# A range flag gathered by a DMA transfer, a fallback program that leaves two engines out, and a last store on another queue

## The chip, the cores and the metric

The kernel runs on one core of a Trainium2 chip, launched as one program. A core has five instruction streams that run on their own and meet through semaphores: TensorE (PE in the profile, with its weight loads as PEld), VectorE (DVE), ScalarE (ACT), GpSimd (POOL) and SyncE (SP), which only issues transfers. The metric is the device time of one execution in microseconds (us); the figure compared is the median of several runs.

## The reference

Two layers follow one another. Inputs are float32: `q`, `k`, `v` of 8 batches x 8 heads x 576 tokens x 64, and the weights of a mixing MLP.

```python
k_p = k.reshape(B, H, 72, 8, D).mean(axis=3)          # pooled keys, 72 of them
v_p = v.reshape(B, H, 72, 8, D).mean(axis=3)
scores = scale * np.matmul(q, k_p.transpose(0, 1, 3, 2))
attn = np.exp(scores - np.max(scores, axis=-1, keepdims=True))
attn = attn / (np.sum(attn, axis=-1, keepdims=True) + 1e-09)
x = np.matmul(attn, v_p)                              # then (B, S, 512)
a1 = alpha1 * x + beta1
u = x + lam * np.einsum('ts,bsd->btd', w_tok, a1)     # mixes the tokens
a2 = alpha2 * u + beta2
out = u + lam * (np.maximum(a2 @ w_ch1, 0.0) @ w_ch2) # 512 -> 2048 -> 512
```

## The kernel before

There are two programs in the kernel. `direct` (line 181) is the fast one. It takes the exponentials without subtracting the maximum, so it is exact enough only while the sums of exponentials stay in a certain range. `general` (line 24) subtracts the maximum, in plain float32, and is there for inputs that leave this range. `tile_pooling_attn__then__resmlp_affine_kernel` (line 1207) runs `direct`, reads a count that `direct` leaves in SBUF into a register of each engine (`values_load`, line 1215), and runs `general` under `tc.If(good < P)` (line 1216). With the inputs measured here the count is 128 and `general` is jumped over: its instructions lie in the instruction streams of the engines, between the last instruction of `direct` and the end of the program, and every engine that takes part in the `If` reads the count, compares and branches past them.

`direct` splits the 8 x 576 tokens into 36 chunks of 128 (the ninth chunk of two batches holds the two remainders of 64 tokens) and the chunks into 9 blocks of four, n = 0 to 8. A block goes through the MLP: `mlp_A` (line 832) makes the hidden layer `H` by 64 products of 128x512 a block, each relu'd by ScalarE (line 850); for blocks from `FIRST` on the second layer is a Winograd-like scheme of seven half-size products instead of eight, with sums of `H` by VectorE (`hidden_sum`, line 925), the products on TensorE (`product`, line 939, line 966) and the sums into the result tile `u_sb` by VectorE (`gather`, lines 981 and 984). While block n is in the MLP, the attention of batch n + 1 runs between its products. The order is written out by hand: each block makes a list `todo` of (due time, step), sorts it and emits the steps in that order (line 1202); inside `direct` the engines keep that order.

The last block, n = 8, has no attention beside it. What matters in its list:

- At 1.5 `all_in_range` (line 227): four VectorE instructions test the reciprocals of all sums (`recs`, 128 x 320) and reduce them to `each`, 128 x 1, one flag in each partition.
- At 7.2 `count_in_range` (line 238): a TensorE product of `each` with a column of ones (`ones_fp`) in a PSUM tile of the pool `gp` gives the number of good partitions, and VectorE converts it to the int32 `count`.
- From 16 on the products, in the order 1, 2, 6, 5, 7, 4, 3, each of the two row pairs `pp` by itself.
- The stores of the result by `store` (line 874), which writes one chunk by one transfer (line 879) or, for the chunk of remainders (m = 3), two transfers of 64 rows (line 883). At 19.1 the left halves of the chunks m = 0 and 1, at 25.2 the right halves of m = 2 and 3, at 27.2 the left halves of m = 2 and 3 (line 1171, one of the 64-row transfers from ScalarE), and at 29.2 the right halves of m = 0 and 1 (line 1173):

```python
todo.append((29.2, lambda m=m: store(
    n, m, HALF, DM, ((nc.sync, nc.scalar)[m],) * 2)))
```

So m = 0 is stored by SyncE's queue and m = 1, the very last piece of the result, by ScalarE's.

Behind the `If` stands the end of the program (all of it recorded under line 1243): SyncE waits for the semaphores of all queues and engines one after another, and the five engines meet twice before the program ends. On the way past the body of the `If` each engine also brings the semaphores that the body would have raised to the value that they would have had (instructions EVENT_SEMAPHORE recorded under line 1216): SyncE those of its eight transfer queues, the others their own.

Of the kernel before, what the change touches and what calls it, by code (L numbers as in the profile page):

```python
# [23 lines left out]
def general(  # L24
# [27 lines left out]
    ident = sb.tile([P, P], FP, tag="ident", name="g_ident")  # L52
    nc.vector.memset(ident, 0.0)
    nc.gpsimd.affine_select(out=ident, in_=ident, compare_op=ALU.not_equal, fill=1.0, base=0,
                            pattern=[[-1, P]], channel_multiplier=1)
    pool = sb.tile([P, 16], FP, tag="pool", name="g_pool")
    nc.vector.memset(pool, 0.125)
    nc.gpsimd.affine_select(out=pool, in_=pool, compare_op=ALU.is_ge, fill=0.0, base=0,
# [3 lines left out]
    pools = sb.tile([P, 5, SPG], FP, tag="pools", name="g_pools")  # L62
    nc.vector.memset(pools, 0.0)
    for c in range(5):
        n = 16 if c < 4 else 8
        nc.vector.tensor_copy(out=pools[:, c, 16 * c:16 * c + n], in_=pool[:, 0:n])

    vec = {}
    for name, src in (("a1", alpha1), ("b1", beta1), ("a2", alpha2), ("b2", beta2), ("lam", lam)):
        vec[name] = sb.tile([P, DM], FP, tag=f"vec_{name}", name=f"g_{name}")  # L70
        nc.sync.dma_start(out=vec[name], in_=src.unsqueeze(0).to_broadcast((P, DM)))
    w1 = sb.tile([P, 4, DFF], FP, tag="w1", name="g_w1")
    nc.sync.dma_start(out=w1, in_=w_ch1.rearrange("(c p) j -> p c j", p=P))
    w2 = sb.tile([P, NJ, DM], FP, tag="w2", name="g_w2")
    nc.sync.dma_start(out=w2, in_=w_ch2.rearrange("(j p) d -> p j d", p=P))

# [6 lines left out]
    for c in range(5):  # L83
        n, rows = tok(c)
        w = sb.tile([P, S], FP, tag="w_tok", name="g_w")
        nc.sync.dma_start(out=w[0:n], in_=w_tok[rows])
        for i in range(5):
            m, cols = tok(i)
            nc.scalar.copy(out=wT[0:m, i, rows], in_=transposed(w[0:n, cols], n, m))

    for b in range(B):
        raw = []
        for src in (q, k, v):
            t = sb.tile([P, 5, H, D], FP, tag=f"raw{len(raw)}", name="g_raw")
            for c in range(5):
                n, rows = tok(c)
                nc.sync.dma_start(out=t[0:n, c], in_=src[b, :, rows].rearrange("h p d -> p h d"))
            raw.append(t)
        means = []
        for t in raw[1:]:  # L100
            ps = ps_l.tile([P, DM], FP, tag="l", name="g_pl")
            for c in range(5):
                n, _ = tok(c)
                nc.tensor.matmul(out=ps[0:SPG], lhsT=pools[0:n, c],
                                 rhs=t[0:n, c].rearrange("p h d -> p (h d)"),
                                 start=(c == 0), stop=(c == 4))
            m = sb.tile([SPG, DM], FP, tag=f"mean{len(means)}", name="g_mean")
            nc.vector.tensor_copy(out=m, in_=ps[0:SPG])
            means.append(m)
        kp, vp = means  # L110
        x = sb.tile([P, 5, DM], FP, tag="x", name="g_x")
        for h in range(H):
            cols = slice(D * h, D * h + D)
            kT = tmp.tile([D, SPG], FP, tag="kT", name="g_kT")
            nc.scalar.copy(out=kT, in_=transposed(kp[:, cols], SPG, D))
            for c in range(5):
                n, _ = tok(c)
                qT = tmp.tile([D, P], FP, tag="qT", name="g_qT")
                nc.scalar.copy(out=qT[:, 0:n], in_=transposed(raw[0][0:n, c, h], n, D))
                sc = ps_s.tile([P, P], FP, tag="s", name="g_sc")[0:n, 0:SPG]  # L120
                nc.tensor.matmul(out=sc, lhsT=qT[:, 0:n], rhs=kT)
                col = tmp.tile([P, 4], FP, tag="col", name="g_col")
                nc.vector.tensor_reduce(out=col[0:n, 0:1], in_=sc, op=ALU.max, axis=AX.X)
                E = tmp.tile([P, SPG], FP, tag="E", name="g_E")
                nc.vector.tensor_scalar(out=E[0:n], in0=sc, scalar1=col[0:n, 0:1], scalar2=None,
                                        op0=ALU.subtract)
                nc.scalar.activation(out=E[0:n], in_=E[0:n], func=AF.Exp, bias=0.0, scale=0.125)
                nc.vector.tensor_reduce(out=col[0:n, 1:2], in_=E[0:n], op=ALU.add, axis=AX.X)
                nc.vector.tensor_scalar(out=col[0:n, 2:3], in0=col[0:n, 1:2], scalar1=1e-9,
                                        scalar2=None, op0=ALU.add)  # L130
                nc.vector.reciprocal(out=col[0:n, 3:4], in_=col[0:n, 2:3])
                ET = tmp.tile([SPG, P], FP, tag="ET", name="g_ET")
                nc.scalar.copy(out=ET[:, 0:n], in_=transposed(E[0:n], n, SPG))
                av = ps_s.tile([P, P], FP, tag="s", name="g_av")[0:n, 0:D]
                nc.tensor.matmul(out=av, lhsT=ET[:, 0:n], rhs=vp[:, cols])
                nc.vector.tensor_scalar(out=x[0:n, c, cols], in0=av, scalar1=col[0:n, 3:4],
                                        scalar2=None, op0=ALU.mult)
        a = sb.tile([P, 5, DM], FP, tag="a", name="g_a")
        for c in range(5):
            n, _ = tok(c)  # L140
            nc.vector.tensor_tensor(out=a[0:n, c], in0=x[0:n, c], in1=vec["a1"][0:n], op=ALU.mult)
            nc.vector.tensor_tensor(out=a[0:n, c], in0=a[0:n, c], in1=vec["b1"][0:n], op=ALU.add)
        aT = sb.tile([P, 4, S], FP, tag="aT", name="g_aT")
        for c in range(5):
            n, rows = tok(c)
            ps = ps_l.tile([P, DM], FP, tag="l", name="g_pl")
            for i in range(5):
                m, _ = tok(i)
                nc.tensor.matmul(out=ps[0:n], lhsT=wT[0:m, i, rows], rhs=a[0:m, i],
                                 start=(i == 0), stop=(i == 4))  # L150
            y = tmp.tile([P, DM], FP, tag="y", name="g_y")
            nc.vector.tensor_tensor(out=y[0:n], in0=vec["lam"][0:n], in1=ps[0:n], op=ALU.mult)
            nc.vector.tensor_tensor(out=x[0:n, c], in0=x[0:n, c], in1=y[0:n], op=ALU.add)
            nc.vector.tensor_tensor(out=y[0:n], in0=x[0:n, c], in1=vec["a2"][0:n], op=ALU.mult)
            nc.vector.tensor_tensor(out=y[0:n], in0=y[0:n], in1=vec["b2"][0:n], op=ALU.add)
            for cc in range(4):
                nc.scalar.copy(out=aT[:, cc, rows],
                               in_=transposed(y[0:n, P * cc:P * cc + P], n, P))
# [9 lines left out]
        for c in range(5):  # L168
            n, rows = tok(c)
            ps = ps_l.tile([P, DM], FP, tag="l", name="g_pl")  # L170
            for j in range(NJ):
                nc.tensor.matmul(out=ps[0:n], lhsT=hid[:, j, rows], rhs=w2[:, j],
                                 start=(j == 0), stop=(j == NJ - 1))
            y = tmp.tile([P, DM], FP, tag="y", name="g_y")
            nc.vector.tensor_tensor(out=y[0:n], in0=vec["lam"][0:n], in1=ps[0:n], op=ALU.mult)
            nc.vector.tensor_tensor(out=x[0:n, c], in0=x[0:n, c], in1=y[0:n], op=ALU.add)
            nc.sync.dma_start(out=out[b, rows], in_=x[0:n, c])


@with_exitstack  # L180
def direct(
# [13 lines left out]
    out: bass.AP,  # L195
    count: bass.AP,
):
# [26 lines left out]

    each = const.tile([P, 1], FP, tag="each", name="each")

    def all_in_range():
# [7 lines left out]
        nc.vector.tensor_tensor(out=ok, in0=ok, in1=flat, op=ALU.mult)  # L235
        nc.vector.tensor_reduce(out=each, in_=ok, op=ALU.min, axis=AX.X)

    def count_in_range():

        ps = gp("ps_ok")  # L240
        nc.tensor.matmul(out=ps[0:1, 0:1], lhsT=each, rhs=ones_fp)
        nc.vector.tensor_copy(out=count, in_=ps[0:1, 0:1])

# [142 lines left out]
    nc.vector.memset(ones_row, 1.0)  # L386
    ones_fp = const.tile([P, 1], FP, tag="ones_fp", name="ones_fp")
    nc.vector.memset(ones_fp, 1.0)

# [734 lines left out]
    for n in range(NBLK):  # L1124
# [27 lines left out]
        if n >= FIRST:  # L1152
# [14 lines left out]
            if last:  # L1167
                for m in range(2):
# [4 lines left out]
                    todo.append((29.2, lambda m=m: store(  # L1173
                        n, m, HALF, DM, ((nc.sync, nc.scalar)[m],) * 2)))
            else:
# [31 lines left out]
def kernel(ctx: ExitStack, tc: tile.TileContext, *args):  # L1207
# [4 lines left out]
    held = ctx.enter_context(tc.tile_pool(name="held", bufs=1))  # L1212
    count = held.tile([1, 1], mybir.dt.int32, tag="count", name="count")
    direct(tc, *args, count)
    good = nc.values_load(count[0:1, 0:1], min_val=0, max_val=P)
    with tc.If(good < P):
        general(tc, *args)
# [30 lines left out]
```

## Time and profile before

| what | value |
|---|---|
| median of 3 runs | 336.12 us (335.84 to 336.51) |
| the profiled execution | 335.74 us |
| its span, first to last instruction of the program | 333.8 us |
| around the span (before and after it) | 1.9 us |
| granted TensorE clock, mean | 0.993 |
| PE busy | 324.6 us (97% of the span) |
| DVE busy | 235.4 us (71%) |
| ACT busy | 175.6 us (53%) |
| POOL busy | 95.2 us (29%) |
| last matmul of the program ends | 327.0 us from the start of the span |
| last VectorE instruction of `direct` ends | 327.4 us |
| SyncE's last wait of the end of the program | 332.8 us |

The page puts register, branch, semaphore and transfer-issuing instructions outside the busy time; they stand in the trace with a "q" behind the engine's name (SPq, ACTq, PEldq), by line. The view of one line lists them by operation, with the shortest, median and longest duration in ns and the times at which the first and the last of them started. The chain of waits goes back from the last busy instruction, which ends at 327.4 us here: what follows it up to 333.8 us has to be read from the lines 1215, 1216, 1243 and from the stores.

### The profile page before, as it was taken

Reading aid. Unit: us, or ns where it says so; the run is one execution under the profiler, and the core shown is the slowest. Engines: PE = TensorE matmul, PEld = TensorE weight load, DVE = VectorE, ACT = ScalarE, POOL = GpSimd, SP = SyncE. Lnnn points to the kernel's source line nnn. Section 1 sums busy time; section 2 is a strip of 40 time slices with the busy share of each in tenths; the row PEclk is TensorE's granted clock in tenths of the full one; section 3 lists DMA queues with packets and bytes.
Section 4 is the critical chain, followed back from the end, with each engine's and each line's share of the span. In section 5 each row is a group of like instructions: output and inputs, shape, how many; then the busy total and the mean of one; then the engine's idle time right before and its main releaser. Section 6 shows DMA issues by size and latency. Waiting matters only on the chain.

```text
span 333.8 us, 6546 instructions
## 1 busy us (share of the span) xinstructions
PE 324.6 (97%) x2533; PEld 209.0 (63%) x2533; DVE 235.4 (71%) x491; ACT 175.6 (53%) x322; POOL 95.2 (29%) x110
## 2 busy tenths in 40 slices
PE   8999999999999999999999999999999999999991
PEld 3668754455445576657675766567756775685681
DVE  6673389899599879686968697769677963354361
ACT  3766989368324842485238613871288127506600
POOL 8769648201264022601170118002700200000000
PEclk9999999999999999999999999999999999999997
DMA  8999999959995971699559933994420044003013
GB/s 121 199 218 270 271 209 253 183 137 135 177 243 86 205 205 38 115 218 157 148 119 229 174 102 81 242 161 143 102 81 2 7 96 103 2 0 128 0 47 91
DMA packets 66480, 45.89 MB, mean 137 GB/s; under 512 B 34397, under 2 KB 57061, under 8 KB 66442
## 3 DMA queue, kind: packets, MB, share of 16 engines
q1 hardware_dynamic: 52092, 32.67, 42.3%
q0 software_dynamic: 13824, 12.40, 22.8%
q8 instruction: 22, 0.36, 0.4%
q10 hardware_dynamic: 526, 0.34, 0.3%
q14 instruction: 16, 0.13, 0.1%
HBM read 38.30 MB, written 9.44 MB: 143 GB/s over the span
## 4 chain that ended last, share of the span: by engine, by line
PE 93%; DMA 2%; POOL 2%; DVE 1%; issue 1%; POOLq 0%
PE ps_h L843 38%; PE ps_w L966 26%; PE ps_tok L795 11%; PE ps_ch L863 8%; PE ps_s L694 2%; PE ps_av L737 2%; DMA q_bf<-in_q_dram 2%; PE ps_r L701 1%; PE ps_av L741 1%; PE ps_kp L626 1%; PE ps_q L583 0%; PE ps_w L510 0%; DVE u_sb L799 0%; POOL k L264 0%; POOL u_bf L805 0%
## 5 line engine op out<-in xcount | busy, mean ns | idle before, releaser
L843 PE MATMUL ps_h<-u_fm,w 128*128 128x512 bf16 (+2 forms) x608 | 133.9, 369 | 0.2 <-DVE bias_cols L846 0.2
L850 ACT ACTIVATE H<-ps_h,bias_cols 128x512 bf16<-128x512 f32 x144 | 98.2, 688 | 56.7 <-PE ps_h L843 55.7
L843 PEld LDWEIGHTS <-w 128*128 128x128 bf16 x608 | 65.6, 114 | 49.5 <-issue 2.2
L966 PEld LDWEIGHTS <-H 128*128 128x128 bf16 x560 | 53.5, 98 | 10.8 <-DVE u_sb L984 1.2
L803 ACT CAST u_bf<-u_sb 128x512 bf16<-128x512 f32 x32 | 19.8, 618 | 70.0 <-issue 39.9
L966 PE MATMUL ps_w<-w_l,H 128*128 128x256 bf16 x448 | 53.6, 273 | 0.0
L984 DVE TENSOR_TENSOR u_sb<-u_sb,ps_w 128x512 f32<-128x512 f32 x54 | 36.3, 683 | 17.0 <-PE ps_w L966 17.0
L759 POOL TENSOR_TENSOR xs<-x_tm,lamal_bc 128x512 bf16<-128x512 f32 x12 | 15.9, 1330 | 108.5 <-DVE x_tm L745 108.3
L795 PE MATMUL ps_tok<-xs,wtT 128*128 128x512 bf16 (+3 forms) x200 | 44.9, 380 | 0.0
L799 DVE TENSOR_TENSOR u_sb<-x_tm,ps_tok 128x512 f32<-128x512 f32 (+1 forms) x40 | 27.3, 684 | 9.9 <-PE ps_tok L795 9.9
L745 DVE TENSOR_TENSOR x_tm<-ps_av,recs 128x320 f32<-128x320 f32 x64 | 31.5, 492 | 2.6
L723 ACT ACTIVATE ET<-ps_s 72x512 f16<-72x512 f32 x56 | 32.3, 592 | 0.0
L795 PEld LDWEIGHTS <-wtT 128*128 128x128 bf16 (+3 forms) x200 | 17.4, 100 | 16.0 <-issue 1.1
L743 DVE RECIPROCAL recs<-ps_av 128x5 f32<-128x5 f32 x64 | 12.1, 189 | 16.7 <-PE ps_av L741 16.4
L664 DVE TENSOR_TENSOR v_u<-v_u 72x1024 f32<-72x1024 f32 (+1 forms) x24 | 22.7, 948 | 0.2
L966 PE MATMUL ps_w<-w_t,h_s 128*128 128x256 bf16 x168 | 22.6, 273 | 0.0
L863 PEld LDWEIGHTS <-H 128*128 128x128 bf16 x128 | 11.9, 98 | 13.7 <-issue 0.4
L364 POOL TENSOR_TENSOR k_raw<-k_raw 128x512 f32<-128x512 f32 x14 | 18.8, 1341 | 1.2 <-DMA k_raw<-in_k_dram 1.2
L966 PEld LDWEIGHTS <-h_s 128*128 128x128 bf16 x168 | 16.4, 98 | 4.1
L366 POOL TENSOR_TENSOR k_bf<-k_raw 128x512 bf16<-128x512 f32 x14 | 18.5, 1319 | 1.1
L935 DVE TENSOR_TENSOR H<-H,H 128x1024 bf16<-128x1024 bf16 x14 | 9.7, 690 | 12.0 <-ACT H L850 11.9
L737 PEld LDWEIGHTS <-ET 72*128 72x128 f16 x256 | 13.9, 97 | 6.3 <-issue 0.3
(156 smaller groups left out, 368.6 us busy)
## 6 DMA issues: line engine op xcount, KB each, us to landing
out_dram<-u_sb SPq DMA_DIRECT2D x29, 256.0 KB
k_raw<-in_k_dram SPq DMA_DIRECT2D x12, 512.0 KB
v_u<-in_v_dram SPq DMA_DIRECT2D x12, 512.0 KB
q_bf<-in_q_dram POOLq DMA_DIRECT2D x16, 256.0 KB, 7.3
w<-in_moe_w_ch_dram POOLq DMA_DIRECT2D x6, 512.0 KB, 13.0
out_dram<-u_sb SPq DMA_DIRECT2D x11, 128.0 KB
w<-in_moe_w_ch_dram POOLq DMA_DIRECT2D x1, 1024.0 KB, 14.4
k_raw<-in_k_dram POOLq DMA_DIRECT2D x2, 512.0 KB, 16.7
```

What stands on the lines that cost most here:

```text
L664: nc.vector.tensor_tensor(out=out, in0=t[:, :, 0:width], in1=t[:, :, width:2 * width], op=ALU.add)
L723: nc.scalar.activation(out=o, in_=i, func=AF.Exp, bias=0.0, scale=0.125)
L737: nc.tensor.matmul(out=av[:, odd + c, :], lhsT=ET[:, m0:m0 + 128], rhs=vp1[:, h % 4, :])
L745: nc.vector.tensor_tensor(out=x[:, 1 - odd:6 - odd, dd:dd + D], in0=av[:, :, 0:64], in1=rec.unsqueeze(2).to_broadcast((P, 5, D)), op=ALU.mult)
L795: nc.tensor.matmul(out=ps_tok[p0:p1], lhsT=wtT[0:kk, at, P * c:P * c + p1 - p0], rhs=xs_pool[i][0:kk, sc, :], start=(sc == 0), stop=(sc == 4))
L799: nc.vector.tensor_tensor(out=s["u"][p0:p1, :], in0=x[p0:p1, 1 + c if c < 4 else 5 - 5 * i, :], in1=ps_tok[p0:p1, 0:DM], op=ALU.add)
L803: nc.scalar.copy(out=s["u_bf"], in_=s["u"])
L843: nc.tensor.matmul(out=ps_h[:, t0:t1 + one], lhsT=w1_of(cc, j), rhs=rhs, start=(cc == 0), stop=(cc == 3))
L850: nc.scalar.activation(out=H4[n, j // 4][:, j % 4, :], in_=ps_h, func=AF.Relu, bias=bias_cols[:, j:j + 1], scale=1.0)
L863: nc.tensor.matmul(out=ps, lhsT=H_of(n, j)[:, 128 * m:128 * m + 128], rhs=(w2l if n else w2)[j // 4][:, j % 4, :], start=(j == 0), stop=(j ...
L966: nc.tensor.matmul(out=ps, lhsT=stat(j), rhs=moving(j), stop=(j == 7), start=(first and (pp == 0 or alone) and j == 0), skip_group_check=True)
L984: nc.vector.tensor_tensor(out=o, in0=o, in1=banks[key, "both"], op=ALU.add)
```

## The change

Four edits. (1) The flags of the 128 partitions are gathered into one row by a transfer from SyncE's queue and reduced there by VectorE; the product, its PSUM tile and the constant column go. (2) The value read is now one flag `fine`, 0 or 1, and it is read by TensorE, ScalarE and GpSimd only. (3) `general` is rewritten so that VectorE and SyncE have no instruction in it: its transfers are issued by GpSimd, its elementwise work is done by GpSimd and ScalarE, the maximum by a tree of subtractions and relus. (4) The store of the right half of m = 1 in the last block goes from ScalarE's to SyncE's queue. The diff, with `general` cut to a few of its lines:

```diff
@@ general
-    nc.vector.memset(ident, 0.0)
+    nc.gpsimd.memset(ident, 0.0)
...
-        nc.sync.dma_start(out=vec[name], in_=src.unsqueeze(0).to_broadcast((P, DM)))
+        nc.gpsimd.dma_start(out=vec[name], in_=src.unsqueeze(0).to_broadcast((P, DM)))
...
-                nc.vector.tensor_reduce(out=col[0:n, 0:1], in_=sc, op=ALU.max, axis=AX.X)
+                while size > 1:
+                    half = size // 2
+                    smaller(low[0:n, 0:half], src[0:n, 0:half], src[0:n, half:2 * half])
...
-            nc.sync.dma_start(out=out[b, rows], in_=x[0:n, c])
+            nc.gpsimd.dma_start(out=out[b, rows], in_=x[0:n, c])
@@ direct
-    count: bass.AP,
+    fine: bass.AP,
...
     each = const.tile([P, 1], FP, tag="each", name="each")
+    every = const.tile([1, P], FP, tag="every", name="every")
...
         nc.vector.tensor_reduce(out=each, in_=ok, op=ALU.min, axis=AX.X)
+        nc.sync.dma_start(out=every, in_=each)

     def count_in_range():

-        ps = gp("ps_ok")
-        nc.tensor.matmul(out=ps[0:1, 0:1], lhsT=each, rhs=ones_fp)
-        nc.vector.tensor_copy(out=count, in_=ps[0:1, 0:1])
+        nc.vector.tensor_reduce(out=fine, in_=every, op=ALU.min, axis=AX.X)
...
-    ones_fp = const.tile([P, 1], FP, tag="ones_fp", name="ones_fp")
-    nc.vector.memset(ones_fp, 1.0)
...
                     todo.append((29.2, lambda m=m: store(
-                        n, m, HALF, DM, ((nc.sync, nc.scalar)[m],) * 2)))
+                        n, m, HALF, DM)))
@@ tile_pooling_attn__then__resmlp_affine_kernel
-    count = held.tile([1, 1], mybir.dt.int32, tag="count", name="count")
-    direct(tc, *args, count)
-    good = nc.values_load(count[0:1, 0:1], min_val=0, max_val=P)
-    with tc.If(good < P):
+    fine = held.tile([1, 1], mybir.dt.int32, tag="fine", name="fine")
+    direct(tc, *args, fine)
+    good = nc.values_load(fine[0:1, 0:1], engines=(mybir.EngineType.PE, mybir.EngineType.Activation, mybir.EngineType.Pool), min_val=0, max_val=1)
+    with tc.If(good < 1):
         general(tc, *args)
```

More of the change, by code (lines that the diff above doesn't have):

```diff
@@ L56, in general @@
     pool = sb.tile([P, 16], FP, tag="pool", name="g_pool")
-    nc.vector.memset(pool, 0.125)
+    nc.gpsimd.memset(pool, 0.125)
     nc.gpsimd.affine_select(out=pool, in_=pool, compare_op=ALU.is_ge, fill=0.0, base=0,
@@ L62, in general, with smaller @@
     pools = sb.tile([P, 5, SPG], FP, tag="pools", name="g_pools")
-    nc.vector.memset(pools, 0.0)
+    nc.gpsimd.memset(pools, 0.0)
     for c in range(5):
         n = 16 if c < 4 else 8
-        nc.vector.tensor_copy(out=pools[:, c, 16 * c:16 * c + n], in_=pool[:, 0:n])
+        nc.gpsimd.tensor_copy(out=pools[:, c, 16 * c:16 * c + n], in_=pool[:, 0:n])
+    minus = sb.tile([P, 1], FP, tag="minus", name="g_minus")
+    nc.gpsimd.memset(minus, -1.0)
+    def smaller(out, a, b):
+        d = tmp.tile([P, SPG], FP, tag="d", name="g_d")[0:a.shape[0], 0:a.shape[1]]
+        nc.gpsimd.tensor_tensor(out=d, in0=a, in1=b, op=ALU.subtract)
+        nc.scalar.activation(out=d, in_=d, func=AF.Relu, bias=0.0, scale=1.0)
+        nc.gpsimd.tensor_tensor(out=out, in0=a, in1=d, op=ALU.subtract)
     vec = {}
@@ L70, in general @@
         vec[name] = sb.tile([P, DM], FP, tag=f"vec_{name}", name=f"g_{name}")
-        nc.sync.dma_start(out=vec[name], in_=src.unsqueeze(0).to_broadcast((P, DM)))
+        nc.gpsimd.dma_start(out=vec[name], in_=src.unsqueeze(0).to_broadcast((P, DM)))
     w1 = sb.tile([P, 4, DFF], FP, tag="w1", name="g_w1")
-    nc.sync.dma_start(out=w1, in_=w_ch1.rearrange("(c p) j -> p c j", p=P))
+    nc.gpsimd.dma_start(out=w1, in_=w_ch1.rearrange("(c p) j -> p c j", p=P))
     w2 = sb.tile([P, NJ, DM], FP, tag="w2", name="g_w2")
-    nc.sync.dma_start(out=w2, in_=w_ch2.rearrange("(j p) d -> p j d", p=P))
+    nc.gpsimd.dma_start(out=w2, in_=w_ch2.rearrange("(j p) d -> p j d", p=P))
     def transposed(src, rows, cols):
@@ L85, in general @@
         w = sb.tile([P, S], FP, tag="w_tok", name="g_w")
-        nc.sync.dma_start(out=w[0:n], in_=w_tok[rows])
+        nc.gpsimd.dma_start(out=w[0:n], in_=w_tok[rows])
         for i in range(5):
@@ L96, in general @@
                 n, rows = tok(c)
-                nc.sync.dma_start(out=t[0:n, c], in_=src[b, :, rows].rearrange("h p d -> p h d"))
+                nc.gpsimd.dma_start(out=t[0:n, c], in_=src[b, :, rows].rearrange("h p d -> p h d"))
             raw.append(t)
@@ L106, in general @@
                                  start=(c == 0), stop=(c == 4))
-            m = sb.tile([SPG, DM], FP, tag=f"mean{len(means)}", name="g_mean")
-            nc.vector.tensor_copy(out=m, in_=ps[0:SPG])
+            m = sb.tile([SPG, H, D + 1], FP, tag=f"mean{len(means)}", name="g_mean")
+            nc.gpsimd.memset(m, 1.0)
+            nc.scalar.copy(out=m[:, :, 0:D], in_=ps[0:SPG].rearrange("p (h d) -> p h d", d=D))
             means.append(m)
@@ L114, in general @@
             kT = tmp.tile([D, SPG], FP, tag="kT", name="g_kT")
-            nc.scalar.copy(out=kT, in_=transposed(kp[:, cols], SPG, D))
+            nc.scalar.copy(out=kT, in_=transposed(kp[:, h, 0:D], SPG, D))
             for c in range(5):
@@ L121, in general @@
                 nc.tensor.matmul(out=sc, lhsT=qT[:, 0:n], rhs=kT)
-                col = tmp.tile([P, 4], FP, tag="col", name="g_col")
-                nc.vector.tensor_reduce(out=col[0:n, 0:1], in_=sc, op=ALU.max, axis=AX.X)
-                E = tmp.tile([P, SPG], FP, tag="E", name="g_E")
-                nc.vector.tensor_scalar(out=E[0:n], in0=sc, scalar1=col[0:n, 0:1], scalar2=None,
-                                        op0=ALU.subtract)
-                nc.scalar.activation(out=E[0:n], in_=E[0:n], func=AF.Exp, bias=0.0, scale=0.125)
@@ L128, in general @@
[L128 to L131, printed above, removed]
+                neg = tmp.tile([P, SPG], FP, tag="neg", name="g_neg")
+                nc.scalar.activation(out=neg[0:n], in_=sc, func=AF.Copy, bias=0.0, scale=-0.125)
@@ new lines, in general @@
+                low = tmp.tile([P, SPG], FP, tag="low", name="g_low")
+                src, size = neg, SPG
+                while size > 1:
+                    half = size // 2
+                    smaller(low[0:n, 0:half], src[0:n, 0:half], src[0:n, half:2 * half])
+                    if size % 2:
+                        smaller(low[0:n, 0:1], low[0:n, 0:1], src[0:n, size - 1:size])
+                    src, size = low, half
+                E = tmp.tile([P, SPG], FP, tag="E", name="g_E")
@@ L132, in general @@
+                nc.scalar.activation(out=E[0:n], in_=neg[0:n], func=AF.Exp, bias=low[0:n, 0:1],
+                                     scale=-1.0)
                 ET = tmp.tile([SPG, P], FP, tag="ET", name="g_ET")
                 nc.scalar.copy(out=ET[:, 0:n], in_=transposed(E[0:n], n, SPG))
[L134 to L137, printed above, removed]
+                av = ps_s.tile([P, P], FP, tag="s", name="g_av")[0:n, 0:D + 1]
@@ new lines, in general @@
+                nc.tensor.matmul(out=av, lhsT=ET[:, 0:n], rhs=vp[:, h])
+                xv = tmp.tile([P, D + 1], FP, tag="xv", name="g_xv")
+                nc.scalar.copy(out=xv[0:n], in_=av)
+                nc.gpsimd.tensor_tensor(out=xv[0:n, D:D + 1], in0=xv[0:n, D:D + 1],
+                                        in1=minus[0:n], op=ALU.pow)
+                nc.gpsimd.tensor_tensor(out=x[0:n, c, cols], in0=xv[0:n, 0:D],
+                                        in1=xv[0:n, D:D + 1].to_broadcast((n, D)), op=ALU.mult)
@@ L140, in general @@
             n, _ = tok(c)
-            nc.vector.tensor_tensor(out=a[0:n, c], in0=x[0:n, c], in1=vec["a1"][0:n], op=ALU.mult)
-            nc.vector.tensor_tensor(out=a[0:n, c], in0=a[0:n, c], in1=vec["b1"][0:n], op=ALU.add)
+            nc.gpsimd.tensor_tensor(out=a[0:n, c], in0=x[0:n, c], in1=vec["a1"][0:n], op=ALU.mult)
+            nc.gpsimd.tensor_tensor(out=a[0:n, c], in0=a[0:n, c], in1=vec["b1"][0:n], op=ALU.add)
         aT = sb.tile([P, 4, S], FP, tag="aT", name="g_aT")
@@ L151, in general @@
             y = tmp.tile([P, DM], FP, tag="y", name="g_y")
[L152 to L155, printed above, removed]
+            nc.scalar.copy(out=y[0:n], in_=ps[0:n])
+            nc.gpsimd.tensor_tensor(out=y[0:n], in0=vec["lam"][0:n], in1=y[0:n], op=ALU.mult)
+            nc.gpsimd.tensor_tensor(out=x[0:n, c], in0=x[0:n, c], in1=y[0:n], op=ALU.add)
+            nc.gpsimd.tensor_tensor(out=y[0:n], in0=x[0:n, c], in1=vec["a2"][0:n], op=ALU.mult)
+            nc.gpsimd.tensor_tensor(out=y[0:n], in0=y[0:n], in1=vec["b2"][0:n], op=ALU.add)
             for cc in range(4):
@@ L174, in general @@
             y = tmp.tile([P, DM], FP, tag="y", name="g_y")
-            nc.vector.tensor_tensor(out=y[0:n], in0=vec["lam"][0:n], in1=ps[0:n], op=ALU.mult)
-            nc.vector.tensor_tensor(out=x[0:n, c], in0=x[0:n, c], in1=y[0:n], op=ALU.add)
-            nc.sync.dma_start(out=out[b, rows], in_=x[0:n, c])
+            nc.scalar.copy(out=y[0:n], in_=ps[0:n])
+            nc.gpsimd.tensor_tensor(out=y[0:n], in0=vec["lam"][0:n], in1=y[0:n], op=ALU.mult)
+            nc.gpsimd.tensor_tensor(out=x[0:n, c], in0=x[0:n, c], in1=y[0:n], op=ALU.add)
+            nc.gpsimd.dma_start(out=out[b, rows], in_=x[0:n, c])
 @with_exitstack
```

## The prediction

> **What bounds the kernel now.** I read the page first for the bound, then the chain of waits over the last 30 us, then, since the chain stops with the last busy instruction, the lines 1215, 1216 and 1243 and SyncE's queue. From the page:
>
> ```profile
> span 333.8 us, 6546 instructions
> PE 324.6 (97%) x2533; PEld 209.0 (63%) x2533; DVE 235.4 (71%) x491; ACT 175.6 (53%) x322; POOL 95.2 (29%) x110
> ...
> PE 93%; DMA 2%; POOL 2%; DVE 1%; issue 1%; POOLq 0%
> ```
>
> TensorE sets the time up to its last product. The change takes almost nothing from TensorE, so what it can do lies in one product and in what follows the last one. The chain of waits, window 305 to 334:
>
> ```profile
> 307.61 0.12 PE ps_ok L241 x2
> 307.73 7.03 PE ps_h L843 x32
> 314.76 12.24 PE ps_w L966 x112
> 327.00 0.02 issue
> 327.02 0.42 DVE u_sb L981
> ```
>
> Two things are to be seen: the flag product (line 241) stands in TensorE's unbroken row, and the chain ends at 327.44 of 333.78 us. The other 6.34 us are in these rows: line 1215, line 1216, line 1243, and the timeline of the last stores (start, duration):
>
> ```profile
> L1215 ACTq TENSOR_LOAD <-count x1: 476/476/476, 327.9 to 327.9; - x1
> ```
>
> ```profile
> L1216 SPq EVENT_SEMAPHORE  x8: 17/17/17, 331.6 to 332.1; - x8
> L1216 POOLq COMPARE_BRANCH  x1: 45/45/45, 308.5 to 308.5; - x1
> ...
> L1216 PEldq COMPARE_BRANCH  x1: 4116/4116/4116, 325.6 to 325.6; - x1
> ...
> L1216 ACTq COMPARE_BRANCH  x1: 58/58/58, 328.5 to 328.5; - x1
> L1216 SPq COMPARE_BRANCH  x1: 58/58/58, 328.8 to 328.8; - x1
> L1216 PEldq EVENT_SEMAPHORE  x1: 51/51/51, 329.8 to 329.8; - x1
> L1216 DVEq EVENT_SEMAPHORE  x1: 21/21/21, 331.0 to 331.0; - x1
> L1216 ACTq EVENT_SEMAPHORE  x1: 17/17/17, 331.5 to 331.5; - x1
> ```
>
> ```profile
> L1243 SPq EVENT_SEMAPHORE  x14: 17/28/28, 332.2 to 333.7; - x14
> ```
>
> ```profile
> 327.02 1.70 SPq L879 DMA_DIRECT2D out_dram<-u_sb  x1
> ...
> 327.47 0.39 ACTq L879 DMA_DIRECT2D out_dram<-u_sb  x1
> ```
>
> The branch past `general` is recorded as 0.05 to 0.07 us on four engines, but the next instruction comes much later: SyncE 328.78 to 331.56 (2.8), ScalarE 328.45 to 331.49 (3.0), VectorE 327.66 to 331.01 (3.4), TensorE 325.58 to 329.76 (4.2). In the packet records an instruction block (8 KB, TensorE 16 KB) is fetched in each gap. GpSimd, whose part of `general` is short, needs 0.19. So the end now is SyncE's: last store issued 328.72, branch to 331.56, eight semaphores to 332.16, twelve waits one after another to 332.90, two meetings of all engines to 333.78.
>
> **The change part by part**, against this execution (span 333.78, time 335.74; the median of 336.12 is 0.38 above it).
>
> *The flag product goes.* Products of line 843 start every 0.216 us; around line 241 the starts are 307.227, 307.658, 307.902, so it costs 0.431 + 0.244 - 2 x 0.216 = 0.24 us (the chain's own row says 0.12, the other end). TensorE waits for nothing from there to 327.0, so all that follows it comes 0.24 earlier: the last gather ends at 327.20.
>
> *The flag by transfer.* `each` is ready at 303.67. SyncE is free from 302.9 to 319.0, so nothing is queued behind the new transfer. No row shows 128 flags of 4 bytes; small transfers of SyncE take 0.54 (line 528) and 0.62 us (line 529) to issue, and line 528's landed 2.4 us after its start. That gives 306.1; a 16 KB fetch at 304.9 to 306.1 may hold one of the 16 parts, 306.5. Lower end 305.6 (a store's 1.97), upper end, for 128 separate pieces, some 312. VectorE waits there for `every`, with `hidden_sum` behind it, due at 308.1 after the shift; it waits 2.2 us for the product today. The reduction (0.49 us for 320 elements) is at most 0.49 against today's 0.15. Even if it came at 312, two sums of 0.69 would be ready by 313.9, before product 1 starts at 314.3, and VectorE idles 2.3 and 2.8 us in between. Cost 0; beyond 312 it would be 1 us for each us.
>
> *`general` rewritten.* None of it runs. GpSimd's body grows, so its branch will cost 2.7 to 4.2 instead of 0.19, from about 307: over by 312, 18 us before it is needed. Removing the constant (0.06 us on VectorE in the first microsecond) is worth 0: the start waits for GpSimd's transfers.
>
> *VectorE and SyncE leave the `If`.* SyncE loses the branch (2.8) and the eight semaphores (0.6), VectorE its 3.4. That is not a gain of 3.4, because SyncE's waits then meet the landing of the last store, 331.23 today, which the branch hides. This is what is late next.
>
> *The last store on SyncE's queue.* Its data is ready at 327.20, its issue adds 0.39 (ScalarE's row) to 0.6 (line 883's longest usual) behind the store of m = 0, whose issue took 1.70 where others take 0.33 to 0.59. Why: TensorE's branch fetches its 16 KB at 326.94 to 328.34, and in that time one of 16 parts of the stores doesn't move (the 9 packets of one part start at 328.33); the issue ends 0.38 after the fetch. The only other long one, line 883 at 205.55 with 1.23, ends 0.37 after a fetch at 205.2 to 206.4. TensorE still branches, so I keep the 1.70: m = 0 issued until 328.48, m = 1 from 328.53, or up to 0.6 later if that part has to drain again. Landing: ScalarE's m = 1 had 15 of 16 parts 1.97 after its start, the last 2.7 after. 328.53 + 1.97 = 330.5; with the later issue 331.1. I take 330.6, near the row. ScalarE gains the issue: its load starts at 326.36 (after its 64-row store), its branch 0.55 later, and 3.04 + 0.08 on it is at the meeting at 330.03; TensorE at 329.67. Both are earlier than 330.6, ScalarE by only 0.6.
>
> *The range check of the register* (0.19 and 0.04 us with gaps 0.39 on SyncE at 308) goes to another engine: 0 on GpSimd, hidden on ScalarE, at most +0.39 if it delays TensorE's fetch.
>
> **Sum.** From the landing: about five waits of 0.06 still stand behind it (now twelve in 0.74), 330.9, then 0.94 from SyncE's last wait (332.83) to the end: 331.9, against 333.78. Gain 1.9: 335.74 - 1.9 = 333.8 for the profiled execution, 336.12 - 1.9 = **334.2** as a median.
>
> [...]
>
> **Rivals.**
> - *The store isn't held* (0.10): if m = 0's issue takes its usual 0.41, both are out by 327.7 and land by 329.9; then ScalarE's branch at 330.03 decides: 330.03 + 0.06 + 0.94 = 331.0, gain 2.7, 333.4. Against it: TensorE's fetch keeps its place relative to the stores.
> - *The second fetch catches the store* (0.17): TensorE fetches the next block too, 330.48 to 331.84, 0.24 earlier then: 330.24 to 331.60. If the part of m = 1 that shares its way is not through by 330.24, it lands at 331.6 + 0.46 (today's end of a packet to its landing) = 332.06; + 0.3 + 0.94 = 333.3, gain 0.45, 335.7. For it: today's part of m = 0 was through at 330.16, only 0.3 before the fetch, and m = 1 is put behind it. Against: ScalarE's store of m = 1 shared the same way, so there are no more packets than before.
> - *Slower: the issue itself is held by the second fetch* (0.07). As m = 0 waits for the first, m = 1 waits for the second: issue ends 331.60 + 0.38 = 331.98, landing 1.5 later (today 328.72 to 330.2) = 333.5, + 0.3 + 0.94 = 334.7: 0.95 slower, 337.1. It decides from the point where m = 1 is not admitted before 330.24; for it only the two long issues speak.
> - *SyncE doesn't get out of the `If`* (0.06), by a branch of its own or by a meeting of all engines ahead of it: issue to 328.92, + 0.06 + 2.8 + 0.6 + 0.74 + 0.88 = 334.0: 336.3, no change.
> - The forecast itself, gain 1.2 to 2.7: 0.60.
>
> **Numbers.** 334.2. The forecast's own range is 333.4 to 334.9; the range with the second fetch's 335.7 and 0.1 to 0.2 of run to run spread at its ends is 333.2 to 335.8, which leaves out the slower case, the unchanged one and a little else. About 0.2% (0.67 us) is what a measurement can tell from no change. Faster by more: 0.60 + 0.10 + a third of the second rival = 0.75; within: the rest of it and the unchanged case, 0.18; slower 0.07.
>
> **What would show it.** Right: no row of lines with the load and the branch for SP and DVE; two stores one after another on SPq at the end, the first with about 1.7; SyncE's waits from about 329 instead of 332; the last of them at about 331 and the span near 331.9; TensorE's products starting every 0.216 us where the flag stood; GpSimd's branch early. Wrong: a transfer of the flag landing after 312 with VectorE waiting, ScalarE or TensorE as the last to meet, a last store landing after 332, or a branch left on SyncE.

## The result, and the profile after

The changed kernel takes 334.24 us (median of 20 runs, 333.24 to 336.47), the kernel before 335.90 beside it (20 runs): ratio 0.9955, 95% interval 0.9934 to 0.9975, so 0.25 to 0.66% faster. The forecast was 334.2. In both kernels some runs, those with a mean clock under 0.9925, are about 2.2 us longer (6 of the 20 here and 13 of 97 of the kernel before in all comparisons, which doesn't settle whether the change makes them more frequent); without them the medians are 333.82 (14 runs) against 335.78 (84 runs), a gain of 1.96.

The page of the changed kernel, then its chain of waits over the window 305 to 334 (start, duration, what):

```profile
span 332.5 us, 6533 instructions
PE 325.2 (98%) x2531; PEld 209.2 (63%) x2531; DVE 236.5 (71%) x490; ACT 175.5 (53%) x322; POOL 95.4 (29%) x110
...
PE 96%; DVE 1%; POOL 0%; issue 0%; ACT 0%
```

```profile
304.82 10.14 PE ps_h L862 x47
314.97 12.24 PE ps_w L985 x112
327.21 0.02 issue
327.23 0.42 DVE u_sb L1000
```

The flag product is gone from TensorE's row. But the last sum ends at 327.65, 0.21 us later than before: this execution was 0.48 us behind already at 14 us, for a reason outside the change (TensorE's clock rose at 6.82 us instead of 4.75, last section), and still 0.46 just before the place of the flag product, where 0.24 was won back. So spans of two single executions mislead by up to half a microsecond here, and from now on I compare the **tail**: from the end of VectorE's last sum to the end of the span. Before: 333.78 - 327.44 = 6.34. After: 332.50 - 327.65 = 4.85. The tail is 1.49 shorter, and 0.24 is won in the body at the flag product.

Line 1235 (the `If`, shortest/median/longest ns, first and last start), line 1234 (the load of the flag), line 1262 (the end of the program) and the last two stores of SyncE:

```profile
L1235 POOLq COMPARE_BRANCH  x1: 45/45/45, 308.1 to 308.1; - x1
...
L1235 PEldq COMPARE_BRANCH  x1: 4129/4129/4129, 326.1 to 326.1; - x1
L1235 ACTq COMPARE_BRANCH  x1: 58/58/58, 327.6 to 327.6; - x1
L1235 ACTq EVENT_SEMAPHORE  x1: 17/17/17, 330.3 to 330.3; - x1
```

```profile
L1234 PEldq FUSED_REGOPS  x1: 165/165/165, 325.8 to 325.8; - x1
L1234 PEldq SEQ_ASSERT  x1: 28/28/28, 326.0 to 326.0; - x1
```

```profile
L1262 SPq EVENT_SEMAPHORE  x13: 17/28/28, 329.8 to 332.4; - x13
```

```profile
L898 SPq DMA_DIRECT2D out_dram<-u_sb x2: 378/1207/2036, 327.2 to 329.4; - x2
```

SP and DVE have no row left under line 1235. SyncE's waits start at 329.8 instead of 332.2. Its second last store is held for 2.04 us, and the range check of the register (FUSED_REGOPS and SEQ_ASSERT), which stood on SyncE, has moved to TensorE. What SyncE waits for in the window 320 to 334 (total, times, longest), before and after:

```profile
SPq L1216 <- SPq L1216: 2.7, 1, 2.7
```

```profile
SPq L1262 <- DMA out_dram<-u_sb: 1.1, 3, 0.5
```

The wait for its own branch is replaced by a shorter one, for the landing of the last stores.

### The profile page after: what moved, and what is told of

The parts are those of the page before. It is cut to its first block, busy times and chain, and to the rows that moved or that the text cites. A ratio compares the mean times of both kernels' runs of the same rounds, so it can differ in the third digit from the quotient of the medians.

```text
span 332.5 us, 6533 instructions
## 1 busy us (share of the span) xinstructions
PE 325.2 (98%) x2531; PEld 209.2 (63%) x2531; DVE 236.5 (71%) x490; ACT 175.5 (53%) x322; POOL 95.4 (29%) x110
## 4 chain that ended last, share of the span: by engine, by line
PE 96%; DVE 1%; POOL 0%; issue 0%; ACT 0%
PE ps_h L862 38%; PE ps_w L985 26%; PE ps_tok L814 11%; PE ps_ch L882 8%; PE ps_av L756 3%; PE ps_s L713 2%; PE ps_warm L805 2%; PE ps_kp L645 1%; PE ps_r L720 1%; PE ps_av L760 1%; PE ps_q L602 1%; PE ps_sc L693 0%; PE ps_w L529 0%; DVE u_sb L818 0%; POOL u_bf L824 0%; PE ps_v L672 0%
```

## The experiments

Each kernel was timed beside the kernel before. The ratio to it is an estimate over all runs with its 95% interval, so it can differ by a little from the quotient of the two medians. The tail comes from one profiled execution of each kernel. In the diffs three dots mark what is left out.

**Parts of the change alone.** The count by product or the flag by transfer, the old or the new second program, the store on ScalarE or SyncE.

`flag_only`: edit 1 alone.

```diff
-        ps = gp("ps_ok")
-        nc.tensor.matmul(out=ps[0:1, 0:1], lhsT=each, rhs=ones_fp)
-        nc.vector.tensor_copy(out=count, in_=ps[0:1, 0:1])
+        nc.vector.tensor_reduce(out=fine, in_=every, op=ALU.min, axis=AX.X)
...
```

> Before, with the flag gathered by the transfer alone (all five engines still read it and take the If, the old second program, the last store on ScalarE). The tail, from the end of VectorE's last sum to the end of the span, is 6.34 us before and 4.85 us after the change. Theory (the end decides, the flag is hidden): products start every 0.216 us throughout, 0.24 us saved, tail still 6.2 to 6.5, median 0.1 to 0.4 below before. Rival (the flag transfer costs): VectorE's next sum of H late and the tail or the products later, median equal or above.

Measured: 335.57 against 335.89, ratio 1.0003 (0.9975 to 1.0030), tail 7.04. No cost of the transfer shows, and no gain that the runs can tell from none. The tail was expected at 6.2 to 6.5. In this profile the held issue is not that of the right half of m = 0 but of the 64-row store before it (1.90 us), so SyncE branches 1.80 after the last sum instead of 1.34, and its branch takes 3.02 instead of 2.79.

`if_only`: edits 2 and 3 alone (new `general`, count read by three engines).

```diff
-    good = nc.values_load(count[0:1, 0:1], min_val=0, max_val=P)
+    good = nc.values_load(count[0:1, 0:1], engines=(PE, Activation, Pool), min_val=0, max_val=P)
...
```

> Before, with the new second program and the count read by TensorE, ScalarE and GpSimd only; the count still comes from the product and the last store stays on ScalarE. Theory (the last engine to meet decides): SyncE is out, and ScalarE becomes the last: last sum 327.44, store to 327.86, load and branch to 328.45, next instruction 3.0 later, tail 5.0 to 5.2, median about 1.2 below before. Rival (SyncE's path alone counts, edit 4 brings nothing): tail 4.4 to 4.85, at or under that of the changed kernel.

Measured: 334.46, ratio 0.9957 (0.9934 to 0.9981), tail 4.92. This is the gain of the whole change. ScalarE's first instruction behind the branch and SyncE's waits:

```profile
L1237 ACTq EVENT_SEMAPHORE  x1: 17/17/17, 333.4 to 333.4; - x1
```

```profile
L1264 SPq EVENT_SEMAPHORE  x13: 17/28/28, 331.5 to 334.4; - x13
```

ScalarE was ready to meet at 333.46 (3.89 after the last sum). SyncE came last, at 333.68: its wait for the last landing (333.17, 3.60 after the last sum) ended at 333.18, and its remaining waits, 0.06 each, followed without a pause. So SyncE's path decided, as the rival had it, though the tail lies 0.07 above the rival's range and 0.08 below that of the theory, and edit 4 has little left to bring.

`store_only`: edit 4 alone.

```diff
-                        n, m, HALF, DM, ((nc.sync, nc.scalar)[m],) * 2)))
+                        n, m, HALF, DM)))
```

> Before, with the last store on SyncE's queue alone. Theory: SyncE still branches, now after two stores, the first held by TensorE's instruction fetch: 328.7 + 0.4 to the branch, 2.8 to the next instruction, then 0.6 + 0.74 + 0.88: tail 6.6 to 6.9, median 0.3 to 0.6 above before. Rival (the landing of the last store decides already before): tail 6.3 as before, median unchanged.

Measured: 336.52, ratio 1.0025 (1.0004 to 1.0045), tail 7.59. Slower alone, as the theory had it, and its tail longer than it had it: SyncE branches at 331.26, 2.1 after the last sum (1.3 before, 1.7 in the expectation), and the branch takes 3.25 this time instead of 2.8.

`store_back`: the changed kernel without edit 4 (the line above reversed).

> The changed kernel with the last store given back to ScalarE. Theory (ScalarE's branch then is the last): tail 5.0 to 5.2 against 4.85, median 0.2 to 0.4 above the changed kernel's, 1.3 to 1.7 below before. Rival (SyncE's last landing decides, and it has one store less): tail 4.3 to 4.6, median below the changed kernel's.

Measured: 334.15, ratio 0.9952 (0.9934 to 0.9971), tail 5.13. The tail is 0.28 longer in the one profile, the times are not to be told apart. The tail is in the range of the theory, but not for its reason: a 64-row store was the held one (2.42 us), the store of m = 0 behind it landed 3.87 after the last sum, ScalarE was ready at the same moment (3.88), and SyncE's last waits followed. No cost of edit 4 shows here, and no gain.

**Where the tail's length comes from.** `no_if`: nothing branches (the way for sums out of range is left out).

```diff
-    good = nc.values_load(fine[0:1, 0:1], engines=(PE, Activation, Pool), min_val=0, max_val=1)
-    with tc.If(good < 1):
-        general(tc, *args)
```

> The changed kernel without the second program, without the load of the flag and without the If (it leaves out the way for sums out of range). No engine branches, so TensorE fetches no block over a branch. Theory (TensorE's fetch holds SyncE's second last store and one share of all stores): that store is issued in 0.35 to 0.6 instead of 2.0 us, the last store lands about 2.4 us after the last sum, tail 3.3 to 3.7. Rival (the hold comes from the stores themselves, too many on one queue): the issue still takes 1.5 to 2.0, tail 4.3 to 4.85.

Measured: 332.65 (4 runs), ratio 0.9881 (0.9834 to 0.9927), tail 3.28. SyncE's last two stores:

```profile
L898 SPq DMA_DIRECT2D out_dram<-u_sb x2: 388/459/530, 326.8 to 327.4; - x2
```

With no fetch by TensorE at the end the issue takes 0.53 instead of 2.04 us and the last store lands 2.11 after the last sum instead of 3.65. The rival (too many stores on the queue) falls: the stores are the same.

`no_pe_if`: ScalarE still branches over a long body, TensorE doesn't (the way for sums out of range is left out).

```diff
...
     with tc.If(good < 1):
-        general(tc, *args)
...
+            for _ in range(2000):
+                nc.scalar.copy(out=t[:, 0:8], in_=t[:, 8:16])
+                nc.gpsimd.memset(t[:, 8:16], 0.0)
...
```

> The changed kernel with another body of the If: 2000 copies of ScalarE and 2000 memsets and eight stores of GpSimd, nothing of TensorE, and the flag read by ScalarE and GpSimd alone (the way for sums out of range is left out). ScalarE branches over a long body, TensorE doesn't. Theory: the issue is not held (0.35 to 0.6), the last landing about 2.4 after the last sum, and ScalarE, 3.0 after its branch at about 327.2, is the last to meet or equal with it: tail 3.5 to 4.0. Rival (any engine's fetch holds the stores in the same way): issue over 1.0, tail over 4.3.

Measured: 333.93, ratio 0.9930 (0.9900 to 0.9960), tail 3.62; issues 0.58 and 0.39, last landing 2.42 after the last sum, ScalarE at the meeting 2.39 after it. Without TensorE's branch the issues aren't held, though ScalarE still branches. Whether a fetch of ScalarE could hold them this kernel doesn't show: its fetch (330.28 to 330.71) began just after both issues had ended (330.24). One part of the 64-row store was late by it all the same: it landed at 331.59, the other fifteen by 330.60.

`no_check`: the range check of the register left out.

```diff
-... min_val=0, max_val=1)
+... min_val=0, max_val=1,
+    skip_runtime_bounds_check_because="a minimum of flags that are 0 or 1")
```

> The changed kernel without the range check of the register, which stands on TensorE now (0.42 us between its load and its branch). Theory: branch, fetch and with them the end of the held issue come 0.4 earlier, issue 1.6 instead of 2.0, tail 4.4 to 4.5, median 0.3 to 0.45 below the changed kernel's. Rival (the hold doesn't hang on the fetch, or the second fetch catches the store): tail 4.85 or more.

Measured: tail 4.34, held issue 1.52:

```profile
L898 SPq DMA_DIRECT2D out_dram<-u_sb x2: 401/960/1520, 327.4 to 329.1; - x2
```

The hold and the tail are close to what the theory said, but only a small part of it for the theory's reason. Against the last sum TensorE's branch comes 0.31 earlier than in the changed kernel, its fetch starts only 0.10 earlier, and the rest of the shorter hold is a shorter fetch: 1.30 us instead of 1.75. Its length differs from profile to profile (1.01 in `copy_base`, 1.40 and 1.68 in the two of the kernel before), so this may be chance. The time does not follow either: 334.45, ratio 0.9934 (0.9907 to 0.9961), an interval that covers most of the changed kernel's. That leaving out the check is faster is not shown.

`all_load`: all five engines read the flag; SyncE and VectorE have no work in the body.

```diff
-    good = nc.values_load(fine[0:1, 0:1], engines=(PE, Activation, Pool), min_val=0, max_val=1)
+    good = nc.values_load(fine[0:1, 0:1], min_val=0, max_val=1)
```

> The changed kernel, but the flag read by all five engines; the second program still has no instruction for VectorE and SyncE. Theory 1 (the If covers the engines that hold the value): SyncE and VectorE branch again, SyncE after both stores, 329.7 + 2.8 + 0.74 + 0.88 (without the eight semaphores, or 0.6 more with them): tail 6.5 to 7.2, median at or above before. Theory 2 (the If covers the engines that have work in its body): only loads are added, tail 4.8 to 5.0, as the changed kernel.

Measured: 334.27, ratio 0.9941 (0.9913 to 0.9970), tail 6.50. Neither theory had it right. The lines of the `If` and of the end of the program, and SyncE's waits:

```profile
L1235 DVEq COMPARE_BRANCH  x1: 72/72/72, 327.5 to 327.5; - x1
...
L1235 SPq COMPARE_BRANCH  x1: 58/58/58, 329.2 to 329.2; - x1
```

```profile
L1262 SPq EVENT_SEMAPHORE  x14: 17/28/28, 329.4 to 333.8; - x14
```

```profile
SPq L1262 <- DMA out_dram<-u_sb: 2.8, 2, 2.3
```

SyncE does branch, at 329.22, and its next instruction starts at 329.42: 0.2 us, not 2.8. VectorE, at 327.54, needs 0.23, and the packet records have no fetch of an instruction block in either gap. So the 2.8 us of the kernel before hang on the body that lies between: there 8 KB blocks are fetched in the gaps (0.31 to 0.77 us each), here none, and reading the flag and branching costs 0.2. The long tail of this one profile is another thing: TensorE's second fetch (329.79 to 331.46) caught a part of a store, which landed at 332.61, 5.28 after the last sum. That is the prediction's second rival, seen at work. It can't come in most executions: the profiled one took 335.99, the median is as low as the changed kernel's.

`before_again`: the kernel before, unchanged.

> The kernel before once more, for the granted clock of each of its runs and a second profile. Expected: tail 6.2 to 7.1 (6.34 in the first profile), its long issue ending 0.36 to 0.44 after TensorE's fetch; runs at a mean clock of 0.983 to 0.988 some 2.2 us above the others, as in the changed kernel, so that this difference has nothing to do with the change.

Measured: 335.82, ratio 1.0004 (0.9976 to 1.0033), tail 6.27; held issue 1.92, its end 0.38 after the fetch (326.45 to 328.13).

**Moving the fetch and the stores.** Three kernels have plain transfers in place of the 50 transposing ones (the transposition is left out of what they compute); what follows the last sum is the same. `copy_base`:

```diff
-            nc.sync.dma_start_transpose(out=u_fm[blk][:, :, 128 * at:128 * at + 128],
-                                        in_=s["u_bf"])
+            nc.sync.dma_start(out=u_fm[blk][:, :, 128 * at:128 * at + 128],
+                              in_=s["u_bf"].rearrange("p (c t) -> p c t", c=4))
... (the same at two other places)
```

> The changed kernel with its 50 transposing transfers replaced by plain transfers of the same tiles (the transposition is left out, so the numbers it computes are other ones). It is the base for the two kernels beside it. Expected: everything after the last sum as in the changed kernel, tail 4.7 to 5.0, the right half of m = 0 held until 0.36 to 0.44 after TensorE's fetch; the body may be some us shorter or longer.

Measured: 334.28, ratio 0.9958 (0.9940 to 0.9977), tail 4.69. Here the fetch (327.87 to 328.88) began 0.8 later against the last sum than in the changed kernel, so m = 0 passed (0.53) and m = 1 was held (1.56), again until 0.38 after the fetch. The expectation that m = 0 is the held one was wrong for this execution: with the fetch 0.8 us later the next store is the one that is caught.

`copy_late8`: the fetch later still.

```diff
+    ps = psB.tile([P, DM], FP, tag="ch", bufs=2, name="ps_late")
+    for _ in range(8):
+        nc.tensor.matmul(out=ps[:, 0:256], lhsT=w2l[0][:, 0, 0:128], rhs=w2l[0][:, 0, 0:256])
```

> The base with plain transfers, and eight more products of 128x256 on TensorE after the last one (their result is used by nothing), so that its load, branch and fetch come about 0.87 us later, while the stores stay where they are. In the changed kernel the fetch begins 0.49 us before the end of VectorE's last sum and holds the right half of m = 0 (2.0 us). Theory: that store is no longer held (0.35 to 0.6); the one of m = 1 is either free or held itself until 0.36 to 0.44 after the end of the fetch; TensorE meets 3.7 after the last sum, tail 4.6 to 5.1. Rival (the hold hangs on the number of stores on the queue): the store of m = 0 still takes 1.5 to 2.0.

Measured: 334.55, ratio 0.9968 (0.9948 to 0.9989), tail 5.15.

```profile
L898 SPq DMA_DIRECT2D out_dram<-u_sb x2: 405/470/536, 327.3 to 327.9; - x2
```

With the fetch at 329.22 to 330.25, after both issues, neither is held. Nothing is won by it: one part of the stores still lands behind the fetch (3.95 after the last sum), and TensorE is the last but one to meet (331.88, 4.11 after the last sum instead of the 3.7 expected).

`copy_swap`: m = 0 from ScalarE, m = 1 from SyncE.

```diff
-                        n, m, HALF, DM)))
+                        n, m, HALF, DM, ((nc.scalar, nc.sync)[m],) * 2)))
```

> The base with plain transfers, and the two last stores dealt the other way round: m = 0, ready 0.87 us earlier, from ScalarE (its branch has 1.3 us to spare), m = 1 from SyncE. Theory: one store less stands before m = 1 on SyncE's queue, its issue ends 0.38 after the fetch, as that of m = 0 does in the base, so its landing and the end come 0.3 to 0.5 earlier: tail 4.3 to 4.6. Rival (what has to pass behind the fetch decides, not the issue): the same bytes, the same tail, 4.8 to 4.9.

Measured: 334.64, ratio 0.9962 (0.9939 to 0.9985), tail 4.52 against the base's 4.69. The profile lies between the two expectations and the times cannot be told apart; whether this order is better stays open. Neither this order nor the later fetch was timed in the kernel with the transposing transfers.

## Why the prediction was right

The terms that carry the forecast of 334.2 (the flag product and the branch that SyncE no longer takes) held: leaving the `If` alone has the gain of the whole change (`if_only`), and what comes late next is the landing of the last stores on SyncE's queue, as forecast. Two sizes were off: the held store was longer, and the body of the profiled execution ended later. That the median is hit to 0.04 us is in part luck. The forecast subtracted a gain of 1.9 from a median of three runs, 336.12. The 20 runs beside the changed kernel have a median of 335.90, and the gain against it is 1.66: a start 0.22 too high and a gain 0.24 too large cancel.

- *Flag product, 0.24.* Matched: the changed execution is 0.46 behind the other up to the flag product and 0.21 behind after it.
- *Flag by transfer, 0.* Its cover held. It was issued at 304.15, fifteen parts landed by 306.07 and the last only at 307.24, behind a fetch (304.25 to 305.65); forecast 306.1 to 306.5. The upper end of 312 was an estimate of mine that no row stood behind. VectorE waited 1.2 us, and the next sum of `H` started 0.46 later than before (308.82 against 308.36), no more than the products were behind.
- *`general` rewritten, 0.* GpSimd's branch took 2.7 (308.12 to 310.85), 20 us before it counts.
- *Leaving the `If`.* The step that carries the gain: `if_only` alone has it all. Its reason was put too broadly. Not taking part saves the 0.2 that a branch with nothing to jump over takes; having no body to jump over saves the rest (`all_load`). So the fourth rival was priced wrongly: a SyncE that branches with nothing to jump over costs 0.2, not 2.8.
- *The held store.* Mis-sized: 2.04 for the 1.70 kept, because the fetch took 1.75 instead of 1.40; what sets its length no run shows. The range check did come to stand on TensorE and its branch came 0.31 later against the last sum, but the fetch began as before, 0.49 ahead of the end of that sum (0.50 before). The mechanism, argued from two stores in the profile before, is now shown: in eleven profiles the long issue at the end stops 0.36 to 0.44 after the end of TensorE's fetch (0.38 in the kernel before, 0.37 in the changed one), and it is absent in the three kernels in which there is no such fetch (issues of 0.53 at most in `no_if`, 0.58 in `no_pe_if`) or it comes after the issues (0.54 in `copy_late8`). Two loads in the profile before show it too, and the prediction left them out: the issues at 157.19 (line 272, 1.61 us) and 223.12 (line 327, 0.96 us) end 0.42 and 0.40 after a fetch.
- *Landing and end.* Forecast: last landing 3.4 after the last sum, tail 4.7. Measured 3.65 and 4.85. The 0.94 from the last wait to the end held to the hundredth. One reading for the second rival is off: the last packet on SyncE's queue ended at 330.76 in the profile before (its landing at 331.23 less the 0.46), not at 330.16, so it was moved during the second fetch (330.48 to 331.84).
- *Where it was off.* The body: forecast 0.24 shorter, in this profile 0.21 longer, because TensorE's clock rose later (at 6.82 us, in the profile before at 4.75); the moment of the rise differs between two profiles of the kernel before as well (4.75 and 5.21). The warm-up products (`ps_warm`) start every 0.427 us before the rise and, in the profile before, every 0.216 us after it; the thirteenth of them starts at 5.65 us in the profile before and at 6.48 in this one, and of these 0.84 us 0.48 are left at 14 us.

## What to carry to other kernels

A conditional block that is never run is paid for by each engine that has a long body in it: here 2.8 us for SyncE and 4.2 for TensorE in the kernel before, 2.5 for GpSimd in `no_pe_if`, 4.5 for TensorE in `if_only`, from the branch to the next instruction, against 0.19 for GpSimd over the short body of the kernel before and 0.20 for SyncE over none in `all_load`. So keep it off the engine that finishes last. Before counting such a gain, ask what the branch hid: here it was the landing of the last stores, which left about 1.5 of the 3.4 us. Compare the stretch that a change touches within each profile, not whole spans, when the time of the start scatters by more than the effect.

## What the runs showed of the hardware

In the changed kernel's profile, with a 16 KB instruction fetch of TensorE from 327.16 to 328.92, one part of sixteen came late in three of the stores under way: fifteen parts of the 64-row store issued at 326.68 landed by 328.60 and the last at 330.53; for the two stores issued at 326.20 it was 328.16 and 330.09, 328.35 and 330.26. SyncE's queue stood too, though no 8 KB block was fetched between 311.96 and 328.57: at one store for 2.04 us, from 327.25 on, and in the other profiles with a held store at the end for 1.52 (`no_check`) to 2.42 us (`store_back`). Not every issue was stopped. With no transfer on its queue in the 2.5 us before it, a store passed in 0.33 us inside a fetch (at 324.45 in the changed kernel's profile, fetch 323.71 to 324.99), and ScalarE's last store passed in 0.39 inside the fetch in the profile before; the held ones had one to four others issued on their queue in that time. What decides was not tested.

TensorE's clock rose at 4.75 and 5.21 us in two profiles of the kernel before and at 6.82 in the changed kernel's, and it stayed up for 324.27 us in all three. In the profile of `if_only` it rose at 4.13, fell again at 10.96 for 6.83 us and then stayed up for 314.03 (columns: window, length, PE, PEld, DVE, ACT and POOL busy, granted clock, DMA share, GB/s):

```profile
4.10:10.90 6.80, 6.12 (x52) 3.19 (x50) 4.29 (x18) 4.28 (x9) 6.72 (x14) 1.00 1.40 191
10.90:17.80 6.90, 6.90 (x69) 5.27 (x67) 4.13 (x12) 4.16 (x12) 4.00 (x6) 0.51 1.21 204
```

What takes the clock back is not shown. In the three profiles with this fall (`if_only`, `store_back`, `copy_swap`: mean granted clock 0.986, 0.986, 0.987) TensorE stood idle for 0.55 to 0.77 us just before its first `ps_q`, from 5.7 to 5.9 us on, but `copy_base` has 0.68 at 6.16 and no fall (0.996).
